# One placing DMA for the spare rows of an output chunk, and a new order of the last two stages

## The chip, the cores and the metric

The kernel runs on one core of one Trainium2 chip. The metric is device time in microseconds (us) of one execution; three runs of the kernel before gave a median of 712.03 us (711.08 to 714.18). A profile of one more execution shows what each engine did: TensorE (PE, with its weight loads as PEld), VectorE (DVE), ScalarE (ACT), GpSimd (POOL) and the queue of SyncE (SP), which issues most of the DMAs. ScalarE issues the others.

## The reference

One input x of 2048 tokens by 640 features goes through two branches, which a gate per token mixes.

```python
g = sigmoid((x * gate_w).sum(-1, keepdims=True))
# branch A: linear attention, 32 heads of 20 features
qkv = (x @ wqkv) ... q, k, v per head
pq, pk = q @ w_phi[h], k @ w_phi[h]
phi_q = concat(softmax(pq), softmax(-pq)); phi_k likewise     # 40 features per head
kv = phi_k^T v;  z = sum_s phi_k
o = (phi_q kv) / (phi_q z + 1e-6)
a = o @ wo
# branch B
b = silu(x @ w1) @ w2                                          # 1728 hidden features
out = g * a + (1 - g) * b
```

All values are float32. Products that must be exact to about float32 are made of three: a value is split into a high part (rounded by ScalarE) and a low part (the difference, by DVE or POOL), and high x high, high x low and low x high are summed (`PASSES`).

## The kernel before

The kernel runs through branch A's keys and values, then the feed-forward branch, then the queries and the output of branch A. The change lies in the last two stages, from about 480 us of the span on.

**The order.** In these stages the work is cut into named operations, and a string lists them (`TAIL` and `FIN`). Each name is popped from a table and issues its instructions at that place; `inorder(PE, DVE, ACT, POOL, SP)` makes every one of the five engines take its instructions exactly in that order. Engines still wait for one another's results, so a name far ahead on one engine can run long after a later name on another. No planner moves anything.

**Chunks.** The queries are handled in eight chunks u of 256 tokens, two tiles of 128 tokens each. Tiles of chunks 0 and 1 belong to `TAIL`; the other twelve are q0 to q11 in `FIN`. The names in `FIN`, b being such a tile:

- `q{b}p` projects the tile (30 matmuls, PE); `m`, `s0`, `s1` take the largest and smallest of each head and subtract (DVE, lines 581 to 588), `e` is the exponential (ACT, line 1334), `S` and `Z` sums (DVE), `z` a multiplication (POOL, line 1351), `P`, `i`, `k` small operations (DVE), `M` the scaling by the weights (POOL, line 1387). `q{b}g` copies the result in 16-bit halves (ACT, lines 1397 and 1401) and issues two DMAs from ScalarE that store it (lines 1402 and 1403).
- `j{u}{k}` loads such a chunk back transposed, with a transposing DMA from SP (line 1415). Chunks 0, 1 and 7 are transposed on PE instead: `t{u}{i}` (line 1641) and the copy `f{u}{i}` (ACT, line 1655).
- `n{u}{i}` multiplies group i of six heads by its block of key-value sums (PE, line 1748); `h` and `l` write the high and low parts of two groups into the tile oT (ACT line 1759, DVE line 1764).
- `z{u}m` does the last two heads, the "rest" (PE, line 1772); `z{u}h`, `z{u}l` split it (ACT line 1778, DVE line 1783); `z{u}s` stores it in a DRAM buffer r_d (two DMAs, line 1788); `z{u}d` places it from there into the spare rows of oT (line 1795).
- `w{p}{m}a`, `w{p}{m}b` are the output matmuls with wo (PE, line 1830), 15 in all for 512 tokens and 128 output features m; p is the oT tile, which holds two chunks (p = 3 and 4 hold one). `y`, `d`, `o`, `c` load the feed-forward part (SP), add (DVE), store (SP) and, for p > 2, gate it (POOL); `gl` loads gates. `x{p}l`, `x{p}s` load (SP) and split (ACT and POOL) the input for later tiles.

In `TAIL`, `fl`, `fm`, `fs` build the fused query weights, `hm`, `hp` and `im`, `ia`, `ig`, `is` finish the feed-forward branch, `qp12` to `qm15` are the four tiles of chunks 0 and 1, `ol`, `os` load and split the five rows of wo, `km`, `kp` are `make_kvw`, and `wa`, `wb`, `W` load weights and gates.

**The spare rows.** A group of six heads gives 120 rows, and an oT chunk has 128. `n_mm` fills it in two halves of 64 partitions (`side`), each of 60 rows from three heads (`KD = 60`) and four rows more, for which `kvw` holds zero columns. So the four spare rows of the first half were partitions 60 to 63 and those of the second 124 to 127. The 40 rows of the rest are laid into these 8 rows of 5 chunks. `r_place` wrote each half's four rows with a DMA of its own, behind the high and low parts of the same rows, and the output matmuls on the tile wait for it. The rows of wo are arranged on the host to match.

Of the kernel before, what the change touches and what calls it, by code (L numbers as in the profile page):

```python
# [76 lines left out]
fl2 hm012 fm0 fl3 fm2 fs0 hp012 fl5 fl1 fs2 fm5 xl0 fl4 fs5 fm1 ol2 fs1 fm4 fm3 fs4 ol1 km fs3 xs0
xl2 qp13 q013 qp12 hm113 q113 hm013 qe13 wa qn13 q012 q112 qN13 qp14 qe12 qs13 hm112 hp013 wb qn12
hp113 W qc13 ol3 os3 qP13 q114 q014 qe14 qi13 qw13 qm13 os2 im0 qs12 os1 ia0 qN12 qs14 qc12 qP12 ol4
qp15 q015 im1 ia1 im2 q115 hp112 os4 qn14 is0 ia2 im3 ia3 im4 ia4 qi12 qe15 qs15 xl1 xs1 im5 ia5  # L80
qn15 is1 qc15 qw12 qN15 qc14 is4 qm12 xs2 im6 qP15 qN14 ol0 ia6 im7 ia7 os0 qP14 qi14 ig6 is6 is2
is3 ig5 im8 kp qw14 qi15 ig7 ia8 im9 ig8 qw15 ia9 qm14 is5 is7 ig9 qm15
# [60 lines left out]
NSEV = (3, 5)  # L143
TPOSE = (0, 1, 7)
FIN = """
y01 x14l x3s x14s q0p x10l q1p q0m q0s1 t05 q0s0 t11 t15 q0e q0z x5l x10s f05 q1m q1s0 f11 t10 z0m
f15 f10 q1s1 x9l t12 t03 z0h z0l f12 q0S f03 z1m z1h z1l x8l q1e t00 t02 t01 f00 q1z q0Z q1S t04 f01
t13 z1s f02 t14 n00 q0P f04 x4s q0i n01 f13 h00 f14 n02 z0s n03 x6l h01 l00 n12 n13 q0k n10 q0M l01
n11 q1Z q1P x15l x5s h10 n04 n14 q1i q2p l10 h02 q1k l02 z0d q1M h11 l11 h12 l12 q3p q2m q2s0 x9s
q0g x6s q1g z1d q2s1 w00a w02a q3m x8s q3s0 x12l w01a w02b q2e q2z q3s1 x11l q2S q3e q2Z x7l j22  # L150
w00b j21 q3z x16l x7s q4p q2P j20 q2i q2k q5p q3Z q3S q3P q3i q3k q4m y00 d00 q2M x11s w01b q2g y02
d02 y03 q3M o00 y04 n22 x13l q4s1 q3g j30 q4s0 z2m q4e j32 n23 j31 q5m n20 n21 q5s0 q4z d01 n24 q5s1
z2h z2l h20 h22 q4S l20 w04a z2s w03a q4Z q5e l22 q5z w04b q4P q4i q4k q4M q5Z h21 x16s q7p n30 n31
q4g o02 q5S d04 q5P z3m z3h l21 n32 q5i q7m z3l q5k q7s0 n33 n34 q5M z3s o04 z2d h30 h32 q7s1 x13s
l30 y10 h31 l32 l31 q7e q7S q6p w03b q7z z3d w14a q5g q6m q6s1 x15s w10a y14 q6s0 q7Z q7P o01 x12s
q6e q6S q6z d03 q7i j41 q7k q7M w14b q6Z q6P y11 q6i q6k w10b x17l q8p q8m j42 d14 q8s1 q8s0 q9p j40
n40 q7g o03 q6M q6g q8e z4m d10 o14 o10 q9m y12 n41 q9s1 q9s0 q9e q8S n42 z4h n43 w12a w12b w11a z4l
q8z w11b j50 q8Z q8P x17s h40 h41 q11p q9z q8i n50 q8k q8M d12 j52 q9Z o12 n44 q8g q9S n51 d11 l41
z5m z5h q9P l40 j51 z4s q9i q9k n52 n53 h42 h51 n54 z5l h50 o11 h52 z5s w13a l42 l52 l50 z4d l51
q10p z5d q11m q11s0 y22 w23a q11s1 q10m w22a q10s1 q9M q10s0 w20a q9g y23 w23b q11e q11S w22b q11z  # L160
q11Z q11P q11i y20 w20b j60 j62 w13b q10e q10S q10z q10Z z6m d22 d23 j61 d20 n62 n63 q10P n60 q10i
q11k q11M n61 z6h n64 y13 z6l w24a q10k q10M o20 d13 h60 h61 h62 o22 o13 y24 w24b w21a l61 o23 t71
f71 t73 f73 t74 l60 f74 z6s t72 t70 t75 w21b f75 y21 l62 n74 d24 o24 z6d f70 n70 n71 z7m y32 f72 n72
n73 z7h d21 z7l gl w34a h70 h72 h71 o21 l72 l71 y34 c32 w30a y30 c30 w30b w32a w34b w32b c34 l70 z7s
z7d d30 o30 y40 d32 y42 w42a d34 o34 o32 w42b w40a w40b y44 c42 d42 c40 d40 c44 o42 w44a w44b d44
o40 o44
"""
ORDERS = (HEAD, O1, O2, O3, O4, O5, O6, O7, O8, O9, O10)
KEPT = (0, 2)
# [5 lines left out]
def mix_kernel(ctx: ExitStack, tc: tile.TileContext, xT, wqT, wkc, wkr, wv, bd, bdc, wo, w1, w1r, w2, out):  # L175
    nc = tc.nc
# [709 lines left out]
    with inorder(PE, ACT, DVE, POOL):  # L886
# [567 lines left out]
    def kvm_load():  # L1454
# [7 lines left out]
        for h in range(n, H):  # L1462
# [2 lines left out]
                kvb["kvm"][k * DH : (k + 1) * DH, 2 * DH * h : 2 * DH * (h + 1)], kv_d[h]  # L1465
            )

    def make_kvw():

        nc.gpsimd.memset(kvw[:, :, KD:], 0.0)  # L1470
        nc.gpsimd.memset(kvwr[:, REST:], 0.0)
        pts = []
        for j0, n in ((0, 8), (8, 3)):
            pt = bank(f"pkvt{j0}", "o")
            pts.append((j0, n, pt))
            for j in range(j0, j0 + n):
                f0, f1 = (j * KF, (j + 1) * KF) if j < 2 * NG else (2 * D - P, 2 * D)
                nc.tensor.transpose(
                    pt[: f1 - f0, (j - j0) * KD : (j - j0 + 1) * KD], kvb["kvm"][:, f0:f1], ident[:KD, :KD]
                )  # L1480
        yield
        for j0, n, pt in pts:
            n = min(n, 2 * NG - j0)
            nc.scalar.copy(kvw[:, j0 : j0 + n, :KD], pt[:GW, : n * KD].rearrange("p (j f) -> p j f", f=KD))
# [50 lines left out]
    with inorder(PE, ACT, DVE, POOL, prev=chain):  # L1535
# [249 lines left out]
    def r_store(u):  # L1785
        _, t = rests.pop(u)
        for k in range(2):
            nc.sync.dma_start(
                r_d[u][:, :, k * P : (k + 1) * P], t[k * CT : k * CT + REST].bitcast(F32)
            )  # L1790

    def r_place(u):
        for side in range(2):
            rows = slice(side * CT + KD, (side + 1) * CT)
            nc.sync.dma_start(
                o_cols(u)[rows].rearrange("r c s w -> r (c s) w").bitcast(F32),
                r_d[u][side * REST // 2 : (side + 1) * REST // 2].rearrange("(r c) s w -> r (c s) w", r=CT - KD),
            )
# [178 lines left out]
```

## Time and profile before

| what | value |
|---|---|
| runs | 712.03 us median of three, 711.08 to 714.18 |
| profiled execution, own time | 711.13 us |
| its span, first to last instruction | 709.4 us |
| its mean granted TensorE clock | 0.995 |
| DVE, ACT, POOL busy | 65%, 43%, 56% of the span |
| issues of a placing DMA | 16, each 40 KB |

A row of a timeline gives the start and the length in us, engine, line, operation and operands, and in brackets how long the engine idled before it and which instruction's end is taken to have released it. Rows of equal kind that follow one another are merged and counted (x30). A wait for several things is put down to the one that came last by the profile; where the engine named had long been done, it was another, often a DMA.

### The profile page before, as it was taken

The numbers are of one execution on the slowest core, as the hardware profiler recorded it, in microseconds if no ns is written. First come the engines' busy times: TensorE is split into PE (matmuls) and PEld (weight loads), VectorE is DVE, ScalarE is ACT, GpSimd is POOL, SyncE is SP. The second block draws the span as 40 slices with busy tenths as digits, with TensorE's granted clock in tenths as the row PEclk, the third lists the DMA queues.
The fourth block names the chain that finished last, engine by engine and source line by source line (L and its number), as shares of the span: only waits on it lengthen the run. The fifth ranks groups of instructions, "written<-read, shape, count | busy, mean of one in ns | idle before, by whom it ended". The sixth has DMA issues, their size and how long they took to land.

```text
span 709.4 us, 11990 instructions
## 1 busy us (share of the span) xinstructions
PE 693.9 (98%) x4536; PEld 589.3 (83%) x4536; DVE 463.8 (65%) x769; ACT 307.8 (43%) x550; POOL 394.5 (56%) x302
## 2 busy tenths in 40 slices
PE   8999999999999999999999999999999989799898
PEld 7888888888888888888888888779889878688678
DVE  4587988886343556678536556566775979858731
ACT  5444454546554243235344423425462844535130
POOL 2367876585653455222875547810499975644332
PEclk9999999999999999999999999999999999899999
DMA  8358878676775567175856643356024388596863
GB/s 313 133 176 305 317 276 318 241 280 227 222 267 167 178 219 244 53 273 198 308 201 218 202 143 120 130 166 211 7 85 147 101 204 215 177 243 163 195 177 117
DMA packets 88631, 140.70 MB, mean 198 GB/s; under 512 B 38466, under 2 KB 52054, under 8 KB 88574
## 3 DMA queue, kind: packets, MB, share of 16 engines
q1 hardware_dynamic: 83134, 132.73, 58.3%
q10 hardware_dynamic: 5440, 7.21, 3.0%
q8 instruction: 36, 0.59, 0.4%
q14 instruction: 21, 0.17, 0.1%
HBM read 87.56 MB, written 45.14 MB: 187 GB/s over the span
## 4 chain that ended last, share of the span: by engine, by line
PE 85%; DVE 5%; DMA 3%; issue 2%; POOL 2%; SPq 1%; ACT 1%; POOLq 0%; DVEq 0%; ACTq 0%
PE o L1196 11%; PE o L1237 11%; PE pa L1830 10%; PE kvp L621 10%; PE a L1107 10%; PE pq L597 8%; PE ph L687 3%; PE b L1107 3%; PE d L1107 3%; PE c L1107 3%; PE o_m L1259 3%; PE hp L706 2%; PE pn L1748 2%; DMA oT<-r_d 2%; PE kvp L492 1%
## 5 line engine op out<-in xcount | busy, mean ns | idle before, releaser
L1227 DVE TENSOR_TENSOR acc<-acc,o 128x512 f32<-128x512 f32 x104 | 68.4, 683 | 35.3 <-PE o L1237 35.2
L621 PE MATMUL kvp<-wh,xa 128*128 128x480 f32 (+2 forms) x420 | 90.2, 357 | 0.1
L1830 PE MATMUL pa<-oT,wo 128*128 128x512 f32 (+1 forms) x375 | 74.4, 357 | 9.4 <-DMA oT<-r_d 6.1
L621 PEld LDWEIGHTS kvp<-wh,xa 128*128 128x128 f32 x420 | 72.7, 188 | 9.8 <-DVE ek L643 0.3
L1196 PE MATMUL o<-u,w 128*128 128x512 f32 x340 | 80.8, 390 | 0.0
L1830 PEld LDWEIGHTS pa<-oT,wo 128*128 128x128 f32 x375 | 61.1, 193 | 21.3 <-DVE sm L1366 4.0
L1196 PEld LDWEIGHTS o<-u,w 128*128 128x128 f32 x340 | 63.7, 188 | 13.6 <-DVE acc L1201 0.3
L1351 POOL TENSOR_TENSOR ez<-eq,zbc 128x1280 f32<-128x1280 f32 x16 | 47.2, 2947 | 35.4 <-ACT eq L1334 26.1
L1123 POOL TENSOR_TENSOR u<-v,u 128x512 fp32r<-128x512 f32 x16 | 20.7, 1293 | 64.1 <-ACT u L1122 64.1
L649 POOL TENSOR_TENSOR ek<-ek,st 128x1280 f32<-128x1280 f32 x16 | 38.2, 2391 | 30.8 <-DVE st L648 13.2
L1121 ACT ACTIVATE v<-v 128x512 f32<-128x512 f32 x33 | 20.9, 632 | 78.4 <-DVE v L1140 36.1
L597 PEld LDWEIGHTS pq<-wq,xb 128*128 128x128 f32 x360 | 53.3, 188 | 1.3 <-issue 0.4
L597 PE MATMUL pq<-wq,xb 128*128 128x320 f32 x360 | 54.3, 310 | 0.0
L1091 POOL TENSOR_TENSOR v<-v,v 128x512 f32<-128x512 f32 x32 | 41.6, 1301 | 13.7 <-DVE u L1123 7.0
L1387 POOL TENSOR_TENSOR eq<-eq,sm 128x1280 f32<-128x1280 f32 x16 | 37.8, 2368 | 18.1 <-DVE sm L1381 17.9
L621 PE MATMUL kvp<-wl,xa 128*128 128x480 f32 (+2 forms) x210 | 47.3, 355 | 0.0
L232 POOL TENSOR_TENSOR xa<-xra,xa 128x512 fp32r<-128x512 f32 (+1 forms) x26 | 28.4, 1114 | 23.5 <-ACT xa L230 22.6
L621 PEld LDWEIGHTS kvp<-wl,xa 128*128 128x128 f32 x210 | 36.6, 188 | 4.5
L1123 DVE TENSOR_TENSOR u<-v,u 128x512 fp32r<-128x512 f32 x25 | 19.9, 797 | 29.5 <-ACT u L1122 29.5
L1107 PE MATMUL a<-xo,wc 128*128 128x512 f32 x132 | 33.5, 389 | 0.0
L1397 ACT COPY ez<-eq 128x2400 uint16<-128x2400 uint16 x10 | 22.0, 2198 | 24.7 <-POOL eq L1387 24.7
L1334 ACT ACTIVATE eq<-eq 128x1280 f32<-128x1280 f32 x16 | 20.4, 1275 | 24.6 <-DVE eq L588 24.6
(253 smaller groups left out, 1551.4 us busy)
## 6 DMA issues: line engine op xcount, KB each, us to landing
w<-w_d SPq DMA_DIRECT2D x20, 640.0 KB
w_d<-aw SPq DMA_DIRECT2D x14, 640.0 KB
sa<-s_d SPq DMA_DIRECT2D x16, 512.0 KB
xr<-xT SPq DMA_DIRECT2D x27, 256.0 KB
m_d<-ez ACTq DMA_DIRECT2D x10, 640.0 KB
ra<-w SPq DMA_DIRECT2D x18, 320.0 KB
wb<-w_d SPq DMA_DIRECT2D x9, 640.0 KB
w_k<-w SPq DMA_DIRECT2D x8, 640.0 KB
```

The lines of the kernel that those rows point to most:

```text
L597: nc.tensor.matmul(dst, xt[c][:, hx, :], w[:, c, hw, lo : lo + n], start=first, stop=(hx == 1 and c == NC - 1))
L621: nc.tensor.matmul(kv_cols(t, lo, hi), xt[c][:, hx, :], WKV[hw][:, c, w_cols(lo, hi)], start=(n == 0), stop=(n == 3 * NC - 1), skip_group_ ...
L649: return lambda: nc.gpsimd.tensor_tensor(groups(e), groups(e), spread(st[:, 1, :]), op=ALU.mult)
L1091: nc.gpsimd.tensor_tensor(v[i], v[a], v[b], op=ALU.subtract)
L1107: last["mm"] = nc.tensor.matmul(out, lhs, rhs, start=(first and i == 0), stop=(stop and i == len(todo) - 1), skip_group_check=True)
L1123: eng.tensor_tensor(u[:, 1, :], v, u[:, 0, :].bitcast(F32), op=ALU.subtract)
L1196: nc.tensor.matmul(o, lhs, rhs, start=(n == 0), stop=(n == len(todo) - 1))
L1227: nc.vector.tensor_tensor(acc[j][m], acc[j][m], o, op=ALU.add)
L1237: nc.tensor.matmul(o, ws[hw], x()[hx], start=(first and i == 0), stop=(i == len(PASSES) - 1), skip_group_check=True)
L1351: nc.gpsimd.tensor_tensor(ez, Q[t]["e"], zbc, op=ALU.mult)
L1387: nc.gpsimd.tensor_tensor(groups(q["e"]), groups(q["e"]), spread(q["sm"][:, 2 * H : 4 * H]), op=ALU.mult)
L1830: nc.tensor.matmul(pa[:, a, :], wo_tile[0][:, c, hw, ds], o[:, c, ho, :size], start=(i == 0), stop=(i == len(TERMS) - 1),)
```

## The change

The second half's columns of `kvw` are moved by four, so that its spare rows come first: partitions 60 to 67 of an oT chunk are then spare, and one DMA places all eight rows. `make_kvw` clears and fills the two halves separately, and the rows of wo are arranged accordingly. `TAIL` and `FIN` list the same operations in a new order.

```diff
     def make_kvw():
-        nc.gpsimd.memset(kvw[:, :, KD:], 0.0)
+        for side in range(2):
+            nc.gpsimd.memset(kvw[:, side::2, spare_of(side)], 0.0)
...
-            nc.scalar.copy(kvw[:, j0 : j0 + n, :KD], pt[:GW, : n * KD].rearrange("p (j f) -> p j f", f=KD))
+            for side in range(2):
+                nc.scalar.copy(
+                    kvw[:, j0 + side : j0 + n : 2, side * (CT - KD) :][:, :, :KD],
+                    pt[:GW, : n * KD].rearrange("p (j f) -> p j f", f=KD)[:, side::2],
+                )
...
+    def spare_of(side):
+        return slice(0, CT - KD) if side else slice(KD, CT)
...
     def r_place(u):
-        for side in range(2):
-            rows = slice(side * CT + KD, (side + 1) * CT)
-            nc.sync.dma_start(
-                o_cols(u)[rows].rearrange("r c s w -> r (c s) w").bitcast(F32),
-                r_d[u][side * REST // 2 : (side + 1) * REST // 2].rearrange("(r c) s w -> r (c s) w", r=CT - KD),
-            )
+        nc.sync.dma_start(
+            o_cols(u)[KD : P - KD].rearrange("r c s w -> r (c s) w").bitcast(F32),
+            r_d[u].rearrange("(r c) s w -> r (c s) w", c=NG),
+        )
...
         "wo": np.concatenate(
             [
-                wo[: NG * GW].reshape(NG, 2, KD, D),
-                wo[NG * GW :].reshape(2, CT - KD, NG, D).transpose(2, 0, 1, 3),
+                wo[: NG * GW].reshape(NG, GW, D)[:, :KD],
+                wo[NG * GW :].reshape(P - GW, NG, D).transpose(1, 0, 2),
+                wo[: NG * GW].reshape(NG, GW, D)[:, KD:],
             ],
```

The two lists are 127 and 473 names long. These are the stretches, by engine, that matter most below:

```text
TensorE, start of FIN to the first output matmul
before  q0p q1p t05 t11 t15 t10 z0m t12 t03 z1m t00 t02 t01 t04 t13 t14 n00 n01 n02 n03 n12 n13 n10 n11 n04 n14 q2p q3p w00a
after   q0p t11 t01 t00 t05 q1p t12 t03 t15 t13 z1m z0m n00 n01 t02 t14 t04 t10 n02 n03 n10 n11 n12 n14 n13 q2p n04 q3p w00a
TensorE, to the first output matmul on chunks 2 and 3, and on chunks 4 and 5
before  q7p n30 n31 z3m n32 n33 n34 q6p w03b w14a ... n54 w13a q10p w23a ... w20b w13b z6m
after   q7p n30 n31 z3m n34 n32 n33 q6p w03a w03b w14a ... n51 q10p w13a w13b w20a
ScalarE, chunks 0 and 1
before  ... f13 h00 f14 h01 x5s h10 h02 h11 h12 x9s q0g x6s q1g x8s q2e
after   ... h00 f04 x5s h10 x7s h01 h12 h11 q0g x9s h02 q1g x8s q2e
SP, chunks 0 and 1
before  z1s z0s x6l x15l z0d z1d x12l x11l x7l j22 j21 x16l j20
after   z1s z0s x8l z0d z1d x12l j20 j21 j22 x13l
SP, chunks 2 and 3
before  y04 x13l j30 j32 j31 z2s o02 z3s o04 z2d y10 z3d y14 o01
after   o00 y04 z2s j30 j32 j31 x15l z3s z2d y14 o01 z3d x16l
SP, chunks 4 and 5
before  y12 j50 j52 o12 j51 z4s o11 z5s z4d z5d
after   y12 j50 j52 j51 z4s y23 y20 z5s o11 z4d o12 z5d gl y22
POOL, TAIL
before  (memsets) xs0 qn13 qn12 os3 qP13 qw13 qm13 os2 os1 qP12 os4 qn14 ... ig7 ig8 qw15 qm14 ig9 qm15
after   os4 qn12 xs2 qn13 os2 xs1 qn14 qP13 os1 (memsets) kp os0 qw13 ... ig5 ig6 ig7 qP15 qw15 qm15 ig9 ig8
```

More of the change, by code (lines that the diff above doesn't have):

```diff
@@ L76 @@
 TAIL = """
[L77 to L82, printed above, removed]
+fl1 xl0 hm012 hp012 fm1 fl2 fm2 ol4 fl5 fl4 fs1 fs2 fm4 fl3 fs4 wa fm0 fm5 fs0 fs5 fm3 W fs3 qp12
+q012 q112 qp13 q013 qe12 os4 qn12 wb hm013 q113 qe13 xl2 qs13 xs2 hm113 hp013 qp14 ol2 q114 q014
+hm112 qs12 qn13 qN13 xl1 os2 xs1 im0 qc13 ia0 qe14 hp113 qn14 qs14 im1 qc12 qP13 qi13 ol1 os1 ol3
+qN12 ol0 km kp qN14 os0 qp15 q015 q115 qw13 hp112 ia1 is0 im2 ia2 qP12 is1 xs0 qi12 is2 qc14 qP14
+qm13 os3 qw12 qm12 qe15 im3 ia3 im4 qn15 ia4 im5 qi14 qw14 qm14 is3 is4 qN15 ia5 ig5 im6 ia6 is5
+qs15 ig6 im7 qc15 ia7 ig7 qP15 qi15 qw15 qm15 im8 ia8 im9 ia9 ig9 is7 ig8 is6
 """
@@ L145 @@
 FIN = """
[L146 to L165, printed above, removed]
@@ L166 @@
-o40 o44
+q0p t11 q0m q0s0 x10l t01 x4s x10s t00 t05 q1p x3s t12 f01 x14l t03 x14s q0s1 q0e q0z q0S f11 t15
+f05 f00 q1m t13 q1s0 f12 x7l f15 z1m z0m n00 f03 z0h q1s1 y03 x5l z1h z1l x6l n01 t02 z0l q0Z t14
+f13 t04 q1e q1z y01 f02 t10 x9l q0P z1s f14 n02 q0i q0k f10 n03 z0s h00 n10 n11 f04 q0M x8l x5s n12
+n14 l00 n13 h10 q1S x7s q2p q1Z n04 h01 h12 q1P h11 q1i q0g q1k q1M x9s l11 h02 l10 l12 l01 l02 z0d
+q1g x8s q2m z1d q2s0 q3p q2s1 q2e q3m q3s0 q3s1 q2S x12l q2z w00a w00b q3e w02a q2Z w02b q2P q2i q2k
@@ new lines @@
+q3S q3z j20 q3Z j21 x6s q3P j22 q4p x13l q3i q3k y02 d02 q2M q2g q5p w01a z2m q4m x11l q3M q4s0 x17l
+n20 o02 q4s1 q5m q3g y00 d00 o00 x11s q4e q4z q5s0 y04 q5s1 n22 w01b z2h z2l n23 z2s n24 n21 w04a
+q5e h20 h22 q4S j30 d01 q4Z q4P q4i q5z j32 q4k l20 h21 l21 w04b q4M q7p q5Z l22 n30 j31 n31 d04
+x13s q5S q4g z3m z3h x15l q5P q5i q5k z3l q7m q5M q7s1 z3s z2d n34 n32 h32 h30 y14 x15s l32 o01 n33
+x12s h31 q6p w03a q5g l30 l31 z3d q7s0 q6m w03b q6s1 q6s0 q7e q7S x16l q6e w14a q7z w10a q6z o04 j41
@@ new lines @@
+q7Z q7P q7i w10b q8p q7k q7M q6S w14b q7g q6Z q6P q6i q6k q6M q9p x17s q8m y11 q8s1 d14 q6g y10 q8s0
+q8e j42 d10 q8z n44 d03 q9m j40 n42 z4m z4h z4l o14 q9s1 n40 n41 h40 n43 h42 h41 o10 w12a w12b o03
+y12 w11a l40 q9s0 q8S w11b x16s q11p j50 j52 j51 q8Z q8P q8i q8k q9e q9z n54 d12 l42 z5m q9Z q9S z4s
+q8M q8g n52 n53 z5h y23 d11 q9P q9i q9k n50 n51 q10p z5l y20 h50 w13a z5s h51 o11 l41 z4d w13b h52
+o12 l50 l51 l52 z5d q11m gl q9M w20a w20b q11s1 y22 y13 q11s0 q10m w23a q9g q10s0 q11e q11z q11S j60
@@ new lines @@
+q10s1 q10e q10S w23b j62 w22a w22b j61 q10z d20 q11Z o20 q11P d23 w24a n60 n61 q11i q11k z6m q10Z
+z6h d22 o22 n62 y24 n63 q10P h60 h61 n64 w24b w21a q10i q10k q10M q11M t73 d13 h62 z6l t71 l62 t72
+f73 f71 t70 t74 f72 o23 z6s y21 t75 l60 w21b y30 c30 n72 l61 z6d d24 d21 n73 f75 z7m f70 n70 o13 f74
+n74 z7h z7l n71 h70 o24 h71 w32a y34 c34 h72 l72 o21 w34a w34b w30a w30b l71 l70 z7s z7d w32b y42
+y32 c42 d34 w40a w42a w42b o34 w40b w44a d30 o30 w44b y40 y44 c32 d32 o32 d42 o42 c40 d40 c44 o40
+d44 o44
@@ L1787, in r_store @@
         for k in range(2):
[L1788 to L1790 removed]
+            nc.sync.dma_start(r_d[u][:, :, k * P : (k + 1) * P], t[k * CT : k * CT + REST].bitcast(F32))
     def r_place(u):
[L1793 to L1798 removed]
+        nc.sync.dma_start(
+            o_cols(u)[KD : P - KD].rearrange("r c s w -> r (c s) w").bitcast(F32),
+            r_d[u].rearrange("(r c) s w -> r (c s) w", c=NG),
+        )
     TERMS = [(c, ho, hw) for ho, hw in PASSES for c in range(NG)]
```

2 lines of the change are left out of this document (1 added, 1 removed).

## The prediction, made before the change was run

> **What bounds the kernel now.** I read the page's engine totals first, then the table of windows over the last two stages, then TensorE's timeline, SP's timeline and the chain that ended last.
>
> ```profile
> span 709.4 us, 11990 instructions
> PE 693.9 (98%) x4536; PEld 589.3 (83%) x4536; DVE 463.8 (65%) x769; ACT 307.8 (43%) x550; POOL 394.5 (56%) x302
> PEclk9999999999999999999999999999999999899999
> ```
>
> TensorE is busy 98% of the span, and its clock row has one digit under 9 before the last column. An edit that moves no matmul can win only the idle places and the slow stretch, so I looked for those where the change works, from 480 us on. In the windows the columns are length, then busy time of PE, PEld, DVE, ACT and POOL, the granted clock, the DMA share and GB/s.
>
> ```profile
> 560.00:580.00 20.00, 17.49 (x103) 15.39 (x100) 16.53 (x28) 11.34 (x15) 15.96 (x10) 1.00 0.65 175
> ...
> 600.00:620.00 20.00, 16.38 (x99) 13.80 (x98) 18.23 (x30) 10.60 (x13) 13.16 (x8) 0.88 0.65 190
> 620.00:640.00 20.00, 20.00 (x117) 17.27 (x116) 11.70 (x19) 7.95 (x9) 9.38 (x4) 0.95 0.94 240
> 640.00:660.00 20.00, 18.13 (x115) 15.35 (x113) 16.13 (x30) 9.09 (x13) 9.79 (x5) 1.00 0.66 177
> 660.00:680.00 20.00, 18.64 (x94) 14.58 (x95) 13.77 (x25) 2.89 (x5) 9.11 (x4) 1.00 0.78 186
> ```
>
> TensorE idles 2.51 us, 3.62 us, 1.87 + 1.36 us here, and the clock drops to 0.88 and 0.95. DVE, with 18.23 of 20 us at its fullest, is the next engine.
>
> ```profile
> 540.95 8.96 PE L597 MATMUL pq<-wq,xb 128*128 128x320 f32 x60
> 560.99 9.06 PE L597 MATMUL pq<-wq,xb 128*128 128x320 f32 x60
> 572.56 8.95 PE L1830 MATMUL pa<-oT,wo 128*128 128x512 f32 x38 [2.51 <-DMA oT<-r_d]
> 606.85 4.66 PE L597 MATMUL pq<-wq,xb 128*128 128x320 f32 x30
> 616.75 9.56 PE L1830 MATMUL pa<-oT,wo 128*128 128x512 f32 x30 [3.62 <-DMA oT<-r_d]
> 653.57 4.57 PE L597 MATMUL pq<-wq,xb 128*128 128x320 f32 x30
> 661.36 12.16 PE L1830 MATMUL pa<-oT,wo 128*128 128x512 f32 x52 [3.23 <-DVE eq L588]
> 688.12 17.93 PE L1830 MATMUL pa<-oT,wo 128*128 128x256 f32 x150
> ```
>
> The bracket is the idle time before a row. All three stand before the first output matmul (line 1830) on a new oT tile: w00a at 572.56, w14a at 616.75, w23a at 661.36. Two are put down to the DMA that places the spare rows. The third names a DVE subtraction into eq, which no operand of w23a reads. SP says what it was:
>
> ```profile
> 563.66 2.80 SPq L1795 DMA_DIRECT2D oT<-r_d  x4
> 608.46 1.34 SPq L1795 DMA_DIRECT2D oT<-r_d  x2
> 610.47 1.27 SPq L1795 DMA_DIRECT2D oT<-r_d  x2
> 652.78 3.17 SPq L1795 DMA_DIRECT2D oT<-r_d  x4
> 692.45 1.36 SPq L1795 DMA_DIRECT2D oT<-r_d  x2
> 565.83 6.59 DMA oT<-r_d
> 611.12 5.54 DMA oT<-r_d
> 616.75 9.56 PE pa L1830 x30
> 637.21 7.07 PE pa L1830 x30
> ```
>
> (Five rows of SP's timeline, four of the chain.) The four placing issues ahead of w23a end at 655.95, 5.4 us before it starts; the two DMA rows of the chain run 6.59 us from 565.83 and 5.54 us from 611.12, each to such a start. I read all three gaps as one thing: the last of four placing DMAs landing late. The last two chain rows show the price of the middle one: thirty output matmuls take 9.56 us right after it and 7.07 us later, so the slow clock costs another 2.49 us. What can be had is 2.51 + 3.62 + 3.23 + 2.49 = 11.85 us. The end is not part of it: the last 150 matmuls run without a break, and what follows them is in both orders the same add and store.
>
> **The change part by part.** The sum is made against the profiled execution, 711.13 us by its own time with a span of 709.36; the median of the runs is 712.03, 0.9 above, and I carry the sum over to the median.
>
> *Merged placing.* Eight pairs of issues become eight issues.
> ```profile
> L1795 SPq DMA_DIRECT2D oT<-r_d x16: 611/647/712, 563.7 to 693.1; - x16
> ```
>
> Each costs SP 0.65 us. Ahead of each late start four issues become two, so the last one ends 1.3 us earlier if it was SP that held it. What flight then remains is not shown. The upper end is the 6.59 us above. The lower end comes from the last two placings: their issue ends at 692.45 + 1.36 = 693.81, and w42a, which needs them, runs inside the unbroken 17.93 us row from 688.12. Ahead of it stand 75 of its 150 half-width matmuls, so it starts at about 697.1: at most 3.3 us. A lone placing may also be slower than either, if eight rows in one DMA cost more (third rival).
>
> *First gap.* In the new order fourteen transposes go ahead of q1p. Their price is in the chain:
> ```profile
> 681.52 2.53 PE pT L1641 x22
> ```
>
> 14 x 0.115 = 1.6 us, so q1p, which ended at 540.95 + 8.96 = 549.9, ends at 551.5. What TensorE does before w00a is the same set, so w00a is reached at 560.99 + 9.06 = 570.05 as before. But n04 now stands behind q2p, and ScalarE's h02 behind q0g and x9s, so a new path sets the placings:
> ```profile
> 549.94 0.82 DVE L581 TENSOR_REDUCE mmq<-pq 128x32 f32<-128x640 f32 x1 [1.25 <-PE pq L597]
> ...
> 552.15 0.81 DVE L588 TENSOR_TENSOR eq<-mmq,pq 128x640 f32<-128x640 f32 x1
> 553.64 1.29 ACT L1334 ACTIVATE eq<-eq 128x1280 f32<-128x1280 f32 x1
> 555.03 2.93 POOL L1351 TENSOR_TENSOR ez<-eq,zbc 128x1280 f32<-128x1280 f32 x1
> 559.42 2.37 POOL L1387 TENSOR_TENSOR eq<-eq,sm 128x1280 f32<-128x1280 f32 x1 [0.22 <-DVE sm L1381]
> 562.25 2.23 ACT L1397 COPY ez<-eq 128x2400 uint16<-128x2400 uint16 x1
> 566.12 0.62 ACT L230 CAST xb<-xrb 128x512 fp32r<-128x512 f32 x1 [1.34 <-issue]
> 560.25 1.63 ACT L1759 CAST oT<-pn 128x512 fp32r<-128x512 f32 x4 [0.61 <-PE pn L1748]
> 563.22 1.34 DVE L1764 TENSOR_TENSOR oT<-pn,oT 128x256 fp32r<-128x256 f32 x3
> ```
>
> From q1p's end: four DVE passes 3.02 (549.94 to 552.96), the exponential 1.29, POOL's q1z 2.93 and q0M 2.37, q0g with its two DMA issues 3.87 (562.25 to the next ScalarE row at 566.12), x9s 0.62, h02 0.41 (a quarter of 1.63), l02 0.45 (a third of 1.34), SP's z0d 0.65. That is 15.6 us, so z1d is issued from 567.1 to 567.75 and w00a waits flight - 2.3 us: 1.0 with 3.3, 4.3 with 6.59. I take 1.6 (flight 3.9), near the lower end, because q0g's large store now leaves some 4 us ahead of z1d, where until now it left beside it. Behind h02 on ScalarE wait q1g and q2e; h02 ends at about 566.0 by this path, and the split after which q1g came until now ended at 566.12 + 0.62, so they are not late.
>
> *Second gap.* w03a now stands behind q6p: 8 matmuls of 7.07/30 = 0.236 us, 1.9 us of cover more. With 1.3 us of issue less the wait is 3.62 - 1.9 - 1.3 = 0.4 at the old flight and nothing at a shorter one. Around it on SP, o04 and y10 leave and y14 and o01 come, one for one. I take 0.2, and 0 for the slow clock. If the cover goes, 3.62 + 2.49 is back.
>
> *Third gap.* Both halves of w13 now stand between q10p and the first output matmul on chunks 4 and 5: 15 x 0.236 = 3.5 us, against a wait of 3.23 less 1.3 of issue. I take 0; it would take a flight of 7.0 us to show again.
>
> *Transposes from memory.* z2s moves ahead of the transposes j30 j32 j31 on SP, and waits there for z2l.
> ```profile
> 592.78 8.11 SPq L1415 DMA_TRANSPOSE fT<-m_d  x3
> ```
>
> They were issued back to back over 8.1 us. Two store issues ahead of them delay the last by 0 to 1.6 us, while TensorE comes 1 us earlier to n32 and n33: a wait of 0 to 2.6 us. I take 0.5, since the second store issue overlaps the time in which the transposes' own inputs land.
>
> *The stage before.* t11 follows q0p directly, at about 545.4, and needs POOL's qm15, which ended only at 549.03:
> ```profile
> 510.99 1.58 POOL L232 TENSOR_TENSOR wo<-wo,wo 128x640 fp32r<-128x640 f32 x1 [5.57 <-ACT wo L230]
> 546.66 2.37 POOL L1387 TENSOR_TENSOR eq<-eq,sm 128x1280 f32<-128x1280 f32 x1
> ```
>
> So 0 to 3.6 us. POOL had 5.57 us idle early, waiting for a wo split. Now the load and split of os4 stand first, ahead of qn12, which fills that hole, and the gate multiplies ig8 and ig9 go behind qm15. 549.03 - 5.57 = 543.5 is before 545.4. I take 0.4. TensorE works without a break there, and the matmuls are only permuted.
>
> *Small parts.* make_kvw's two copies become four and one memset two:
> ```profile
> 535.14 0.71 ACT L1484 COPY kvw<-pkvt 120x480 f32<-120x480 f32 x2
> ```
>
> That is 0 to 0.7 us on ScalarE, which idles elsewhere; kp now comes right behind km and frees two banks 20 us sooner. Below nothing is possible too. If ScalarE's slack is gone, im3 waits for a bank by as much. I take 0. The rows of wo are permuted before the launch, and matmuls, stores and bytes stay.
>
> *Sum.* After: 1.6 + 0.2 + 0 + 0.5 + 0.4 = 2.7 us of waits where 11.85 stood; gain 9.15. 711.13 becomes 702.0, the median 712.03 becomes 702.9.
>
> [...]
>
> **The rivals.** *First: the first gap grows.* The path of 15.6 us stands, but the flight stays 6.59, because reloads and the store still crowd the queues. Then w00a waits 4.3 us, over the 3.62 that brought the slow clock, and pays 2.5 more: 6.8 for 1.6, 708.1. For it: each flight that set a start was 5.4 to 6.6 us. Against: the store now leaves earlier. [...]
>
> *Second: the wait moves to the transposes.* If z2s holds SP until j31 is 4 us late, n32 waits 4 us and the clock drops: 6.5 instead of 0.5, 708.9, which a measurement cannot tell from before. For: SP serves strictly in order, and three transposes already took 8.1 us. Against: q2g and q3g, which they read, are not earlier than before, so z2s fills a wait.
>
> *Third: slower.* One DMA over eight rows lands later than two over four. The three waits are then flight - 2.3, - 5.1 and - 7.0 us, with 2.5 us of clock for each over 3.6. The change breaks even at about 7.5 us (5.2 + 2.5 + 2.4 + 0.5, and 0.9 elsewhere); at 9 us it gives 6.7 + 2.5 + 3.9 + 2.5 + 2.0 + 0.9 = 18.5, so 718.7. For: a flight does depend on how much is in the queues (3.3 against 6.59). Against: no row reaches 7, and the bytes stay.
>
> **How the numbers follow.** Forecast 0.62, first rival 0.15, second 0.13, third 0.08, and 0.02 for less than 700, where more goes than the three gaps. From no change a measurement here tells about 0.5%, 3.6 us, so up to 708.5 is faster: 0.62, 0.02 and 0.10 of the first rival, 0.74. The rest of it and the second make 0.18 for no change, the third 0.08 for slower. Low is 712.03 - 11.85 = 700.2, rounded to 700; high takes in both rivals near 708 to 709: 709.4. The forecast's own range is 700.5 to 705.5.
>
> **What would show it.** Right: the clock row has no dip near 620 us, L1795 has eight issues of about 0.65 us, the first output matmuls after q6p and q10p have no bracket over 0.5 us, the one after q3p has 1 to 2.5 us, and the span is 698 to 703. Wrong: a bracket over 3.5 us before w00a with a slow stretch behind it; n32 or t11 waiting over 2 us; or placings that land over 7 us after their issue.

## The result, and the profile after

The changed kernel takes 703.29 us, the median of four runs (702.29 to 704.52), where the kernel before takes 711.56 us (710.83 to 714.18, four runs). The ratio is 0.987, 95% interval 0.9851 to 0.989. The forecast was 702.9. The profiled execution is the slowest of the four, 704.52 us by its own time. Two executions of the experiments below, one of 761.36 us at a granted clock of 0.852 and one of the kernel before of 1771.89 us, are in the slow state and are left out of the ratios.

From the page of the changed kernel: the span, the engines' totals, the clock row, and the group of the output matmuls (now line 1834; behind the first bar the group's busy time and the mean of one, behind the second the idle time just before the group).

```profile
span 702.6 us, 11974 instructions
PE 694.7 (99%) x4536; PEld 589.1 (84%) x4536; DVE 464.4 (66%) x769; ACT 309.4 (44%) x552; POOL 395.5 (56%) x303
PEclk9999999999999999999999999999999999999999
L1834 PE MATMUL pa<-oT,wo 128*128 128x512 f32 (+1 forms) x375 | 73.8, 354 | 2.3 <-DMA oT<-r_d 2.3
```

TensorE's timeline of the changed kernel, the rows that answer to those of before:

```profile
547.49 4.65 PE L597 MATMUL pq<-wq,xb 128*128 128x320 f32 x30
573.02 8.71 PE L1834 MATMUL pa<-oT,wo 128*128 128x512 f32 x30 [2.10 <-DMA oT<-r_d]
615.67 5.52 PE L1834 MATMUL pa<-oT,wo 128*128 128x512 f32 x23 [0.21 <-DMA oT<-r_d]
652.63 15.74 PE L1834 MATMUL pa<-oT,wo 128*128 128x512 f32 x68
```

The windows of the same kernel (length, busy time of PE, PEld, DVE, ACT, POOL, granted clock, DMA share, GB/s):

```profile
560.00:580.00 20.00, 17.90 (x100) 15.08 (x97) 18.21 (x29) 11.39 (x15) 15.98 (x10) 0.91 0.55 140
600.00:620.00 20.00, 19.79 (x121) 16.84 (x120) 17.81 (x30) 10.10 (x12) 13.48 (x7) 1.00 0.83 219
620.00:640.00 20.00, 20.00 (x123) 17.29 (x122) 16.64 (x28) 9.99 (x12) 13.10 (x7) 1.00 1.07 261
```

Of the three waits before a first output matmul on a new tile, the one of 3.62 us has become 0.21 and the one of 3.23 has gone (the row at 652.63 has no bracket). The first, 2.51 before, is still 2.10. The slow clock has moved: 1.00 near 620 us now, 0.91 near 570, where the thirty matmuls from w00a on take 8.71 us. The kernel before needed 7.07 for thirty at full clock, so this stretch, at 0.80 of the clock over its 8.71 us, costs 1.64. After: 2.10 + 0.21 + 1.64, and 0.31 before a group of transposes, make 4.26 us where 11.85 stood, 7.6 less; the span fell by 6.8, and the work ahead of these two stages, which the change does not touch, ended 0.84 later in this execution (their first matmul starts at 479.70, before at 478.86). The medians fell by more, 8.3 us, since the profile after is of the longest of its four executions.

### The profile page after: what moved, and what is told of

Same layout as the page of the kernel before. It is cut to its first block, busy times and chain, and to the rows that moved or that the text cites. A ratio compares the mean times of both kernels' runs of the same rounds, so it can differ in the third digit from the quotient of the medians.

```text
span 702.6 us, 11974 instructions
## 1 busy us (share of the span) xinstructions
PE 694.7 (99%) x4536; PEld 589.1 (84%) x4536; DVE 464.4 (66%) x769; ACT 309.4 (44%) x552; POOL 395.5 (56%) x303
## 4 chain that ended last, share of the span: by engine, by line
PE 95%; DMA 2%; DVE 1%; ACT 1%; SPq 0%; issue 0%; DVEq 0%; ACTq 0%
PE kvp L621 18%; PE o L1196 11%; PE o L1237 11%; PE pa L1834 10%; PE a L1107 10%; PE pq L597 9%; PE ph L687 3%; PE b L1107 3%; PE c L1107 3%; PE d L1107 3%; PE o_m L1259 3%; PE pn L1756 2%; PE hp L706 2%; PE kvt L608 2%; DMA oT<-r_d 1%; PE kvp L492 1%
## 5 line engine op out<-in xcount | busy, mean ns | idle before, releaser
L451 ACT COPY v<-kvp 128x340 f32<-128x340 f32 (+1 forms) x30 | 12.4, 423 | 40.8 <-PE kvp L621 22.1
```

## The experiments

All were timed in five rounds. The kernel before gave 711.71, 711.02, 711.5 and 711.92 us beside them; each ratio is against the one timed beside it, and medians of different sets are compared only roughly. First theory: the gain is the merged DMA, which lands earlier. Rival: the gain is the order, which puts matmuls between the placing and its reader.

**The merge alone.** The changed kernel with both old lists (`TAIL` and `FIN` of before).

> Old orders of both stages, only the merged placing. Theory A, the gain is the three placing waits and the merge alone takes most of them: z1d is issued 1.2 us earlier and its flight falls from 6.6 to about 4.9 us (as in the changed kernel), so the waits before w00a, w14a and w23a become 0 to 0.5, 1.4 and 1.1 us instead of 2.51, 3.62 and 3.23, no slow clock: 702.5 to 705 us. Rival B, the new order does it by putting work between, and the merge only saves SP issues of which SP has plenty: 708 to 711 us.

702.92 us, ratio 0.9873 (0.9853 to 0.9894): all of the gain. TensorE's timeline of this kernel:

```profile
569.86 8.87 PE L1834 MATMUL pa<-oT,wo 128*128 128x512 f32 x38
604.08 4.66 PE L597 MATMUL pq<-wq,xb 128*128 128x320 f32 x30
612.38 8.72 PE L1834 MATMUL pa<-oT,wo 128*128 128x512 f32 x30 [2.02 <-DMA oT<-r_d]
```

No wait at w00a (569.86), none at w23a, and 2.02 at w14a with a slow stretch behind it (8.72 for thirty, at 0.80 of the clock).

**The order alone.** The kernel before with both new lists, so two DMAs on four rows each.

> New orders of both stages, but two placing DMAs of four rows each as before. Theory A: the last of four placings lands about 2 us later than in the changed kernel each time, so the waits are about 4.1 us before w00a with the slow clock behind it, 1.4 before w14a and 1 to 2 before w20a: 708 to 711 us. Rival B: the order covers the waits by itself, 703 to 705 us.

711.79 us, ratio 1.0008 (0.9989 to 1.0026): nothing. TensorE's timeline of this kernel, then a row of SP's:

```profile
564.92 0.65 PE L1748 MATMUL pn<-fT,kvw 120*64 120x256 f32 x4
574.57 9.51 PE L1830 MATMUL pa<-oT,wo 128*128 128x512 f32 x30 [4.41 <-ACT eq L1334]
620.89 7.00 PE L1830 MATMUL pa<-oT,wo 128*128 128x512 f32 x23 [3.08 <-issue]
665.22 13.89 PE L1830 MATMUL pa<-oT,wo 128*128 128x512 f32 x53 [2.28 <-DVE eq L588]
```

```profile
566.48 2.71 SPq L1795 DMA_DIRECT2D oT<-r_d  x4
```

n04, which now stands behind q2p, ends at 565.57, and the first placing is issued at 566.48 where it was 563.66: w00a waits 4.41 instead of 2.51. The other two waits are shorter than before, but slow stretches stand behind all three (9.51 us for thirty, 7.00 for 23 and 13.89 for 53, where the kernel before takes 7.07 for thirty at full clock). The three waits sum to 9.77 us where they were 9.36: what the order saves at the second and third tile it spends at the first. This profile is of the second longest of twelve executions (715.33 us, granted clock 0.990, where those at the median have 0.995), so it shows more of the slow clock than the median has. Theory A's waits of 1.4 and 1 to 2 us came out larger, and the median is 0.8 above its range.

**The changed kernel with the old `TAIL`.**

> The changed kernel with the old order of TAIL alone; FIN and the merged placing stay new. If the new TAIL is there to have POOL done earlier: t11 stands right behind q0p, at about 546, but POOL's qm15 ends near 549 in the old order, so TensorE waits about 3 us before t11, perhaps with the slow clock: 706 to 709 us. If the order of TAIL does not matter: 703.3 us as the changed kernel.

707.64 us, ratio 0.9942 (0.9923 to 0.996). TensorE's timeline:

```profile
549.23 2.47 PE L1649 MATMUL pT<-ident,eq 128*120 128x128 f32 x12 [2.89 <-POOL eq L1387]
551.35 5.41 PE L597 MATMUL pq<-wq,xb 128*128 128x320 f32 x30
577.60 7.11 PE L1834 MATMUL pa<-oT,wo 128*128 128x512 f32 x30 [2.07 <-DMA oT<-r_d]
```

Transposes wait 2.89 us for POOL's qm15, with a slow stretch behind (q1p takes 5.41, in the changed kernel 4.65; the clock is 0.50 from 549.60 to 553.00 us). At w00a the wait is 2.07 and the clock full (1.00 from 577.60 to 584.70 us). The new `FIN` needs the new `TAIL`.

**The new `TAIL` with the old `FIN`, merged.**

> Merged placing, the new order of the stage before the last (the list TAIL) with the old order of the last stage (FIN). Theory A (the two orders fit each other, as the changed kernel with the old TAIL lost 4.3 us): 705 to 709, with a wait among the transposes or ahead of w00a. Theory B (the new TAIL is good or bad by itself, and it was not bad in the changed kernel): 701 to 703.5.

701.56 to 703.26 us, ratio 0.9876 (0.986 to 0.9892): as with both old lists, and theory B. No row is shown, since the profile is of the execution of 761.36 us. So, by the times alone, the new `TAIL` is worth something only where the new `FIN` asks for qm15 early.

**The gap at w00a filled.** The changed kernel with eight matmuls of ones into w00a's bank, which w00a then overwrites.

```diff
+        if (p, m0, k) == (0, 0, 0):
+            for i in range(8):
+                nc.tensor.matmul(pa[:, 0, :]..., ones, ones[...]..., start=(i == 0), stop=(i == 7))
         for a, i in todo[half * k : half * (k + 1)]:
```

> The changed kernel with eight more matmuls of ones (512 columns, 0.236 us each) into w00a's bank just before w00a, which fill the 2.10 us in which TensorE waits for the placing; the real matmuls overwrite them. If the idle time is what brings the slow clock (30 matmuls in 8.71 us instead of 7.07): granted clock 1.00 behind it and 0 to 1.6 us less, 701.7 to 703.3 us. If the slow clock there has another cause: clock still under 1 after w00a, and 703.3 us.

701.79 us, ratio 0.986 (0.9839 to 0.9881), 1.5 below the changed kernel. TensorE's timeline:

```profile
570.21 2.02 PE L1833 MATMUL pa<-ones 128*128 128x512 f32 x8
572.40 7.11 PE L1843 MATMUL pa<-oT,wo 128*128 128x512 f32 x30 [0.18 <-DMA oT<-r_d]
```

Counted from the end of q3p the reader starts no earlier (2.2 us behind it, in the changed kernel 2.1), but runs at full clock: 7.11 us for thirty matmuls instead of 8.71. So at this place the idle time brings the slow clock, and its price is 1.6 us by the two traces. The medians agree with that, but their ratios overlap.

**One step of cover on the merged kernel.**

```diff
-... z2h z2l h20 h22 q4S l20 w04a z2s w03a q4Z ... q6p w03b q7z z3d w14a
+... z2h z2l h20 h22 q4S l20 w04a z2s q4Z ... q6p w03a w03b q7z z3d w14a
```

> Merged placing with both old orders, and one step of the last stage moved: w03a stands right behind q6p, ahead of w03b, and no longer ahead of q4Z. Theory A (the placing for w14a waits for a chain that starts on PE ahead of q6p, so 1.9 us of matmuls moved from in front of that chain to behind it cover the 2.02 us wait that the merged kernel with the old orders still has; the half clock behind that wait, some 1.6 us, goes with it): wait at w14a under 0.4 us, clock full there, 699.0 to 700.5 us. Theory B (the chain to the placing hangs on VectorE or POOL and not on PE, so the placing is issued no earlier): the wait stays at 1.5 us or more, 702 to 703.5.

701.06 us, ratio 0.9856 (0.9843 to 0.9869), between the two theories. TensorE's timeline:

```profile
597.24 4.67 PE L597 MATMUL pq<-wq,xb 128*128 128x320 f32 x30 [1.12 <-DVE sm L1381]
612.91 7.13 PE L1834 MATMUL pa<-oT,wo 128*128 128x512 f32 x30 [0.42 <-DMA oT<-r_d]
```

The wait at w14a falls from 2.02 to 0.42 and the clock is full there (7.13 us for thirty), as theory A had it. But w03a had been covering something where it stood: the projection after it (q7p) now waits 1.12 us for a sum of DVE. 1.60 + 1.6 - 1.12 = 2.1 by the traces. The medians of the two kernels differ by 1.9, but their ratios overlap (0.9853 to 0.9894 and 0.9843 to 0.9869).

**The cover alone, without the merge.** On the kernel before, w03a behind q6p, and w13a and w13b between q10p and w23a.

> The kernel before, two DMAs on four rows each, with the cover of the prediction alone: w03a moved right behind q6p, and w13a and w13b moved between q10p and w23a. The rest of both orders is the old one. Theory A (cover does what the prediction counted): the wait at w14a falls from 3.62 to some 1.7, the one at w23a from 3.23 to 0, the one at w00a stays 2.5; 5.1 us gained, and up to 2.5 more if the half clock behind w14a goes: 704 to 706.6. Theory B (moved matmuls move the issue of the placing too, so the waits stay): 709.5 to 712.

707.5 us, ratio 0.9941 (0.9927 to 0.9955), 0.9 above the range of theory A. TensorE's timeline:

```profile
571.99 10.55 PE L1830 MATMUL pa<-oT,wo 128*128 128x512 f32 x38 [2.15 <-DMA m_d<-ez]
600.26 4.67 PE L597 MATMUL pq<-wq,xb 128*128 128x320 f32 x30 [1.12 <-DVE sm L1381]
616.53 7.12 PE L1830 MATMUL pa<-oT,wo 128*128 128x512 f32 x30 [1.01 <-DMA oT<-r_d]
658.56 10.55 PE L1830 MATMUL pa<-oT,wo 128*128 128x512 f32 x45 [1.49 <-DVE eq L588]
```

The second wait fell as counted and more, to 1.01. But 3.5 us of matmuls took only 1.74 off the third (3.23 to 1.49), q7p waits 1.12 again, and there is a slow stretch behind w00a (10.55 for 38, 8.87 in the merged kernel; the clock is 0.84 from 571.90 to 582.60 us).

**Why the merge saves more than its issues: five ways to cut a placing.** A placing is eight rows of ten pieces of 1 KB. All of these have the old orders, and differ in the DMAs of `r_place` (the last also has the old layout). Two halves of the columns, all eight rows:

```diff
+        for c in (slice(0, NG // 2), slice(NG // 2, NG)):
             nc.sync.dma_start(
-                o_cols(u)[KD : P - KD].rearrange("r c s w -> r (c s) w").bitcast(F32),
-                r_d[u].rearrange("(r c) s w -> r (c s) w", c=NG),
+                o_cols(u)[KD : P - KD, c].rearrange("r c s w -> r (c s) w").bitcast(F32),
+                r_d[u].rearrange("(r c) s w -> r c s w", c=NG)[:, c].rearrange("r c s w -> r (c s) w"),
             )
```

> The merged kernel with the old orders, but each placing is split again into two DMAs: both on all eight rows, each on half of the columns. Same bytes, same number of issues as before, but eight rows in each. Theory A (what the merge saves is the second issue, 0.68 us of SP, and little more): w14a's wait 2.7 us, the other two waits at most 0.7: 703 to 705.5. Theory B (the number of DMAs costs more than its issue, since each further DMA on the queue lands later by itself): the waits of before come back, 707 to 711. Theory C (four rows against eight is what counts): as the merged kernel, 702.3 to 703.5.

Four DMAs of 3, 3, 2 and 2 pieces a row (`[:, 0:3]`, `[:, 3:6]`, `[:, 6:8]`, `[:, 8:10]` on both sides):

> The merged kernel with the old orders, each placing split into four DMAs on all eight rows, of 24, 24, 16 and 16 KB. Theory A (SP's time for a DMA goes with the pieces of each row, ten of them here, and not with the number of DMAs): the four issues take 0.65 to 0.7 us together, as the one and the two did; waits as with two halves (1.3 us at w14a) or less, 699.5 to 701.2. Theory B (each issue has a fixed part that shows once the pieces are few): four issues take 1.3 us or more, waits at w14a 2 us or more, 702 to 706.

Four DMAs of two rows with all ten pieces (rows `r` to `r + 2` for r = 0, 2, 4, 6):

> The merged kernel with the old orders, each placing split into four DMAs on two rows each, of 20 KB, with all the columns. Theory A (a DMA's issue takes SP 0.68 us for ten pieces a row, whether it has two, four or eight rows): 2.7 us of issue for each placing where two four-row DMAs took 1.36 and one of eight rows 0.69; the waits come back larger than in the kernel before (5 us at each of the three placings, with half clocks behind them): 714 to 720. Theory B (the issue goes with the bytes, or the rows are spread wider): 1.36 us or less for the four, 703 to 712.

And the kernel before, with nothing of the change, its two four-row DMAs cut after the fourth piece:

```diff
-        for side in range(2):
-            rows = slice(side * CT + KD, (side + 1) * CT)
-            nc.sync.dma_start(o_cols(u)[rows]..., r_d[u][...]...)
+        for c in (slice(0, 4), slice(4, 10)):
+            for side in range(2):
+                rows = slice(side * CT + KD, (side + 1) * CT)
+                nc.sync.dma_start(o_cols(u)[rows]...[:, c]..., r_d[u][...]...[:, c])
```

> The kernel before (old layout, old orders), each of its two four-row DMAs split by columns, into 16 KB and 24 KB, the first columns of both halves ahead of the others. So four DMAs for each placing, as with the quarters (24, 24, 16, 16 KB), and about the same SP time, 1.2 to 1.3 us; only the rows of each differ, four here, eight there. [...] Theory B (what counts is that the pieces of a DMA are few and the first columns land first): waits as with the quarters, about 1 us at w14a and none else, 700.4 to 702.5; then the eight adjoining rows were not needed.

In the view of the tile oT from 600 to 620 us, the placing issues have one row each: their number, then the shortest, median and longest time of SP in ns. The kernel before:

```profile
L1795 SPq DMA_DIRECT2D oT<-r_d x4: 611/628/654, 608.5 to 611.1; - x4
```

The merged kernel:

```profile
L1799 SPq DMA_DIRECT2D oT<-r_d x2: 668/676/684, 605.7 to 607.0; - x2
```

Two halves of the columns:

```profile
L1800 SPq DMA_DIRECT2D oT<-r_d x4: 264/282/304, 605.0 to 606.5; - x4
```

Quarters:

```profile
L1800 SPq DMA_DIRECT2D oT<-r_d x8: 269/298/303, 606.1 to 608.9; - x8
```

Four-row halves in the old layout:

```profile
L1796 SPq DMA_DIRECT2D oT<-r_d x8: 245/298/313, 605.7 to 608.5; - x8
```

The starts of q6p and w14a in TensorE's timeline, in the kernel with two halves:

```profile
603.36 4.67 PE L597 MATMUL pq<-wq,xb 128*128 128x320 f32 x30
610.94 7.12 PE L1835 MATMUL pa<-oT,wo 128*128 128x512 f32 x30 [1.29 <-DMA oT<-r_d]
```

With quarters:

```profile
604.50 4.67 PE L597 MATMUL pq<-wq,xb 128*128 128x320 f32 x30
611.75 7.13 PE L1835 MATMUL pa<-oT,wo 128*128 128x512 f32 x30 [0.96 <-DMA oT<-r_d]
```

With two-row DMAs:

```profile
611.18 4.66 PE L597 MATMUL pq<-wq,xb 128*128 128x320 f32 x30
623.59 8.98 PE L1835 MATMUL pa<-oT,wo 128*128 128x512 f32 x30 [6.13 <-DVE sm L1371]
```

With four-row halves:

```profile
604.11 4.67 PE L597 MATMUL pq<-wq,xb 128*128 128x320 f32 x30
611.72 7.29 PE L1831 MATMUL pa<-oT,wo 128*128 128x512 f32 x30 [1.33 <-DMA oT<-r_d]
```

In the table, the time of SP is the median issue times the number of issues. The two columns "landed" give when the DMA with the columns that w14a's first matmul reads, and when all of the placing, had landed: the last semaphore update of the DMA in the trace.

| a placing's DMAs | SP, one issue (us) | SP, one placing (us) | after q6p's start (us): first columns landed | all landed | w14a starts | median (us) | ratio, 95% |
|---|---|---|---|---|---|---|---|
| 2 x 4 rows x 10 pieces (before) | 0.63 | 1.26 | 9.81 | 9.81 | 9.90 | 711.56 | |
| 1 x 8 rows x 10 (merged) | 0.68 | 0.68 | 8.16 | 8.16 | 8.30 | 702.92 | 0.9873 (0.9853 to 0.9894) |
| 2 x 8 rows x 4, 6 | 0.28 | 0.56 | 7.44 | 7.71 | 7.58 | 700.58 | 0.9852 (0.9839 to 0.9865) |
| 4 x 8 rows x 3, 3, 2, 2 | 0.30 | 1.19 | 7.11 | 7.85 | 7.25 | 700.95 | 0.9856 (0.9835 to 0.9877) |
| 4 x 4 rows x 4, 6 (old layout) | 0.30 | 1.19 | 7.48 | 8.15 | 7.61 | 701.62 | 0.986 (0.9838 to 0.9882) |
| 4 x 2 rows x 10 | 0.60 | 2.4 | 12.32 | 12.32 | 12.41 | 722.05 | 1.0152 (1.0131 to 1.0172) |

(The two-row issues take 599/600/672 ns in the same view; TensorE waits 3.90, 6.13 and 5.49 us at the three tiles there, and the matmuls behind take 11.46 us for 38, 8.98 for 30 and 14.71 for 52.) The two halves came out below all three of their ranges: no theory had a second cut doing better than one DMA. The quarters lie in theory A's range, the two rows 2 us above theory A's, the four-row halves in theory B's. Three things follow.

- The time of SP for an issue does not go with the rows or the bytes: 20, 40 and 80 KB in ten pieces a row have medians of 0.60 to 0.68 us, and in these views every DMA of two to six pieces a row takes 0.24 to 0.31, whether it is 16 KB or 48 (over the whole program a few take longer, up to 0.72). The reason that the quarters' theory A gave fell there: four issues take 1.2 us, not 0.65.
- SP's time does not set the wait either. The kernel before and the four-row halves use SP for 1.26 and 1.19 us a placing, and w14a starts 2.3 us earlier with the halves.
- Eight adjoining rows were not needed: four-row halves in the old layout and the old orders gain as much as the merge (0.986 against 0.9873). Against quarters with eight rows, they wait 1.33 and not 0.96; the cut differs too, so at most 0.4 us goes to the rows.

So short DMAs, with the columns first that are read first, are what the wait answers to. The part of the order shows in the chain of the two-halves kernel:

```profile
606.17 4.63 DMA oT<-r_d
```

The DMA that released w14a is the one whose issue began the pair at 606.17, the first half: the first output matmul no longer waits for the last column. By the columns "landed" that is worth 0.27 us with two halves, 0.74 with quarters and 0.67 with four-row halves. The rest is that the whole placing lands earlier, by 0.45 us with two halves against one DMA, and by 1.66 with four-row halves against the kernel before. Why it does stays open: the two DMAs ahead of w14a landed 5.18 and 5.54 us after their issues began in the kernel before, and the four DMAs that they are cut into landed after 3.63 to 3.73, issued in the same time.

**Both together.** The changed kernel with both its orders, each placing in two halves of the columns.

> The changed kernel with both its orders, its placing split into two DMAs on all eight rows, 48 KB and 32 KB. Theory A (two DMAs of eight rows take no more of SP than one and land some 0.6 us earlier, as with the old orders): the wait at w00a falls from 2.10 to 1.5, the one at w14a from 0.21 to 0; with the half clock behind w00a (1.64 us) still there 702.2 to 702.9, without it 700.5 to 701.3. Theory B (the gain with the old orders had another cause): waits of 2.1 and 0.2 again, 703 to 704.5.

700.33 us, ratio 0.9845 (0.9824 to 0.9866), the fastest median here. TensorE's timeline:

```profile
570.70 7.16 PE L1835 MATMUL pa<-oT,wo 128*128 128x512 f32 x30
608.44 8.87 PE L1835 MATMUL pa<-oT,wo 128*128 128x512 f32 x38
648.75 15.74 PE L1835 MATMUL pa<-oT,wo 128*128 128x512 f32 x68
```

No wait is left at the three tiles and no slow stretch (the clock is 1.00 from 478 us to the end), where theory A still had 1.5 us at w00a. It beat the kernel before. Against the changed kernel the trace shows the 3.95 us of waits and slow clock gone and the median is 3.0 lower, but the ratios, taken beside different sets, overlap slightly (0.9851 to 0.989). They do not set it apart from the halves with the old orders either (0.9839 to 0.9865), so the new orders are worth nothing that shows here.

## Why the prediction was right, and where it was not

*The time.* 702.9 was forecast and 703.29 measured, but that they lie so close is in part luck. The gain was forecast at 9.1 us and is 8.3; the base of 712.03 (three executions) was 0.5 above the 711.56 of four, two terms of the sum were off in opposite directions, and the credit was shared out wrongly.

*Merged placing: mis-sized.* I counted its worth as 1.3 us of issue at each wait, and left the rest to cover. The merge alone took off 2.51, 1.60 and 3.23 us. At w14a the count was nearly right: the last issue moved from 4.27 us behind q6p's start (611.12 - 606.85) to 2.90, 1.37 earlier, and the flight fell by 0.28, as these rows of the chain and of SP in the merged kernel show:

```profile
606.98 5.26 DMA oT<-r_d
```
```profile
563.63 1.58 SPq L1799 DMA_DIRECT2D oT<-r_d  x2
605.70 0.68 SPq L1799 DMA_DIRECT2D oT<-r_d  x1
647.56 2.24 SPq L1799 DMA_DIRECT2D oT<-r_d  x2
```

At w23a it was far off: the last issue ends at 649.80, and w23a starts at 652.82 without a wait, where before 5.4 us lay between the two. I held the old flight fixed there. By the semaphore updates of the traces it fell from 5.93 us behind the start of the issue to 3.56, and at w00a from 6.59 to 4.90. At these two tiles the shorter flight gives more than the saved issues, and why it is shorter is the question left open above.

*Cover: counted twice.* The terms of 1.9 and 3.5 us stand in the sum beside a merge that already removes most of the waits. Alone they gain 3.5 us (711.02 to 707.5). With the merge, the first is worth about 2 by the traces and the second nothing, since that wait is gone.

*First gap: the path right, the clock wrong.* I had z1d issued from 567.1 to 567.75 and a wait of 1.6. These rows of the changed kernel (the timeline of several engines, then one row of the chain) show the path:

```profile
565.67 0.65 PE L1756 MATMUL pn<-fT,kvw 120*64 120x256 f32 x4
565.70 0.62 ACT L230 CAST xb<-xrb 128x512 fp32r<-128x512 f32 x1 [1.06 <-issue]
566.37 0.37 ACT L1767 CAST oT<-pn 128x256 fp32r<-128x256 f32 x1
566.77 0.42 DVE L1772 TENSOR_TENSOR oT<-pn,oT 128x256 fp32r<-128x256 f32 x1 [0.61 <-ACT oT L1767]
567.22 1.50 SPq L1799 DMA_DIRECT2D oT<-r_d  x2
```
```profile
568.05 4.83 DMA oT<-r_d
```

n04 behind q2p and x9s end together at 566.32, h02 and l02 follow, and z1d is issued from 568.05 to 568.72. It lands 4.2 us after its issue, where I took 3.9, and w00a waits 2.10. The failed step is the clock behind it, which the sum does not have: the prediction charged the slow clock only to waits over 3.6 us, an estimate from one wait with it (3.62) and one without (3.23), and put nothing behind this one. It cost 1.64. A smaller slip: the 6.59 us of the chain's row run from the start of the issue, and the formula "flight - 2.3" from its end, 0.63 later. On one footing the upper end was 5.96 us, and a wait of 3.7 and not 4.3. The merged kernel with the old orders has no wait here, so the new `FIN` makes this gap, and that it would was in the prediction, but not that the merge alone would do without it.

*The rest.* The second and third gaps came out at 0.21 and 0 for 0.2 and 0. No transpose from memory and no t11 waits, where I had 0.5 and 0.4; instead 0.31 stands at a group of transposes behind a copy of ScalarE. That the new `TAIL` is needed for t11 is borne out by the 2.89 us with the old one. The copies of `make_kvw` cost nothing that shows.

*The rivals.* The first (a long flight at w00a) did not happen as it was told, since the flight was 4.83 and not 6.59; but its slow clock came: 2.10 and 1.64, 3.7 us for its 6.8. The second did not happen. The third, a slower DMA over eight rows, did not: its flights are 4.83 and 5.26 where those of four rows were 5.54 and 6.59.

*The flight.* The sum took 3.9 us, near a lower end of 3.3 that came from the last two placings. Counted from the end of the issue it is 4.2 us ahead of w00a in the changed kernel and 4.6 ahead of w14a in the merged one; only ahead of w23a in the merged kernel is it 2.9. The 722.05 us with two rows do not speak for the number of rows: the last DMA ahead of w14a flies 5.59 us there, and 5.54 with four rows, but four issues take 2.4 us where two took 1.26. From four rows to eight, in short DMAs, the rows are worth 0.4 us at most.

## What to carry to other kernels

When a small DMA is late, cut it along its columns before changing the layout to merge it, and send first what is read first; for the time of the issuing queue, count pieces per row and not rows or bytes (here 0.60 to 0.68 us an issue with ten pieces, 0.24 to 0.31 with two to six). When a change has two parts that answer to the same wait, run each alone: here one had all of the gain and the other none, and the sum came out right because one term too small met another counted twice. A wait of 2 us on TensorE may cost a second time in clock (2.10 us cost another 1.64 here), so fill it or remove it, and look at the clock behind it.

## What the hardware showed that was not expected

The length of a wait did not tell here whether the clock drops behind it. By the windows or the time of the matmuls behind it, it dropped behind waits of 2.02, 2.10, 2.15, 2.28, 2.89, 3.08, 3.62, 3.90, 4.41, 5.49 and 6.13 us, and stayed full behind 2.07, 2.51 and 3.23. Two rows of the windows show it, the changed kernel behind 2.10 us and the one with the old `TAIL` behind 2.07 (the clock is the number ahead of the last two):

```profile
573.02:581.73 8.71, 8.71 (x32) 7.01 (x33) 8.42 (x14) 1.78 (x2) 8.45 (x4) 0.80 0.79 188
```
```profile
577.60:584.70 7.10, 7.10 (x32) 5.86 (x33) 6.93 (x11) 1.79 (x2) 6.87 (x4) 1.00 0.78 176
```

At half speed for t and full for the rest, 0.80 over 8.71 us makes t = 3.5 us, an estimate; the windows of the same kernel give 0.50 from 573.69 to 577.10 us, and 1.00 on both sides of it. Behind the 2.02 us of the merge alone the windows give 0.80 from 612.38 to 621.10 us, and behind the 2.15 of the cover alone 0.84 from 571.90 to 582.60.

In the profiles of the kernel before and of the changed one, the clock behind a wait goes with where the wait falls. The slow stretches there run from 615.17 to 622.00 us and from 573.69 to 577.10 us, so they last 6.83 and 3.41 us, one twice the other. Cut into pieces of 3.41 us, counted both ways from the start of the slow stretch, the windows from 480 to 700 us give a clock of 1.00 or 0.50 in every piece and nothing between. These are the pieces with the waits in them:

| kernel | wait (us) | window (us) | TensorE busy in it (us) | clock in the next |
|---|---|---|---|---|
| changed | 2.10 | 570.28 to 573.69 | 1.31 | 0.50 |
| before | 3.62 | 611.76 to 615.17 | 1.37 | 0.50 |
| before | 3.23, second part | 659.55 to 662.96 | 1.60 | 1.00 |
| before | 2.51 | 570.80 to 574.21 | 1.65 | 1.00 |
| before | 3.23, first part | 656.13 to 659.55 | 2.00 | 1.00 |

Every other piece at full clock has 2.66 us of work or more, and half clock follows none of them. So the wait of 2.10 us, inside one piece, was followed by a slow stretch, and the one of 3.23 that two pieces share was not. Two drops in two profiles show no rule; that the place of a wait, and not its length, brings the drop is the author's reading of these rows. Executions of one kernel differ too: those of the changed kernel have granted clocks of 0.998, 0.999, 1.0 and 0.998, and the one at 1.0 is the fastest, 702.29 us. A single profile does not tell whether a wait of 2 to 3.2 us will cost clock.

The other surprise is SP's time for an issue: about 0.65 us for ten pieces a row and 0.3 for six or fewer; no placing of seven to nine pieces was run.
